# A Fourier mixing layer with a low-rank mixer: narrow products put side by side in four groups of partitions, and two small copies moved ahead of the weight loads

## The chip, the cores and the metric

The kernel runs on one core of one Trainium2 chip. The metric is device time in microseconds of one launch. The engines are named as the profile names them: PE is the matmul engine, with PEld for its loads of the stationary operand; DVE, ACT and POOL are the vector, scalar and general engines; SP issues DMAs. A matmul `out <- moving, stationary` of "98*128 98x425" contracts 98 partitions, has 128 stationary columns and 425 moving columns.

## The reference

For eight batches of 3136 positions by 256 channels:

```python
X = np.fft.fft(x, axis=1); X = np.fft.fft(X, axis=2); x = X.real     # (8, 3136, 256)
xt = x.transpose(0, 2, 1)
h = xt @ U @ V                          # over positions, rank 32
u = x + h.transpose(0, 2, 1)
out = u + np.maximum(u @ w_ch1, 0.0) @ w_ch2    # 256 -> 1024 -> 256
```

## The kernel before

**Transform.** The real part of the two-dimensional transform is written as cosine and sine sums. Per batch, DVE folds x over channels (`along_d`, L348) and over positions (`mirror`, L357; `half`, L361) into two tables `G` (`g`, one for each parity `par` of the output position). PE multiplies their columns with the position tables `tabs` (sine, typ 0) and `tabc` (cosine, typ 1) in `seq` (L423): one call for each parity, type and parity `pn` of the contracted position, each of four products of 425 moving columns: 393 output positions and 32 columns that carry the low-rank factor U. `halves` (L390) does a call with `pn` 0 from products of 229 columns and two DVE operations that make the rest of it by symmetry. ACT copies the `pn` 0 result to `ev`, and DVE adds and subtracts it to the `pn` 1 result, giving the arrays `A` (cosine) and `B` (sine) and the slice `tab` for the low rank. `even_ch`, `odd_ch` (L552, L561) transform over channels and make `S` and `T`; `across` (L569, L571) copies what is left over into `VA`. `lowrank` (L579) makes `TA`. PSUM tag `dft` with three buffers serves all of these.

**The channels that the folding leaves over.** Channel 0 folds with nothing and stands alone. For batches 0 and 1 it is column 256 of `G`, copied there by way of POOL (`alone`, L354), and its position transform is carried by four more products in each call of `seq` with typ 0 (L421), which add it as row 0 of `B`. With those, batch 1 can't use `halves` for typ 0. For the six batches from 2 on the channels are loaded apart by SP (`column_loads`) and transformed together in the *column pass* (`column_steps`): `fold_c` makes tables `GC`, `group` (L511) runs four times, for each `par` and `pn`, with four products of 6 stationary columns each, and `finish` makes `rows` and the low-rank part `tabc128`.

**Mixer.** The 25088 rows are taken in 49 chunks of 512. `front` (L612, L620) makes u; `first_product` (L632) and a ReLU on ACT (L634) make `h`; `second_product` (L648) and DVE (L654 to L657) make the output, which SP stores.

**Order.** Up to the end of chunk 0 everything is queued in the order in which it is written; after it a scheduler orders the instructions within engines, from a list `due` that spreads the steps of batch b+1's fold and transform over the chunks of batch b. In the setup, tables are made by ACT, POOL and DVE; `transform_u` (L274) already has 32-column products that write four groups of 32 partitions of one PSUM tile:

```python
nc.tensor.matmul(acc[g * R:(g + 1) * R, :], GU[:kp(i), typ, pn, i, :], ...)   # L274, g in range(4)
```

POOL's order around the moved copies is: four `mirror_even` copies (L309), `load_weights` (L55 gather of w, L195), `cosine_odd(4)` (L323), `alone(0, ...)` twice (L354), `load_v`, `g_zeros(0)`, batch 1's first load, `ta_rows`, `alone(1, ...)` twice, memsets, and later `channel_tables` (L807), which scales row 0 of `MC`.

Of the kernel before, what the change touches and what calls it, by code (L numbers as in the profile page):

```python
# [10 lines left out]
BF16 = mybir.dt.bfloat16  # L11
# [5 lines left out]
P = 128  # L17
# [10 lines left out]
def kernel(  # L28
# [153 lines left out]
    MSN = cpool.tile([P, 256], BF16, name="msn")  # L182
    MC = cpool.tile([P, 256], BF16, name="mc")
    ME = cpool.tile([P, P], BF16, name="me")
    MO = cpool.tile([P, P], BF16, name="mo")
    nc.vector.tensor_scalar(ncol[:], ncol[:], 1.0 / S, 0.0, op0=AL.mult, op1=AL.max)

    w1 = [gen.tile([P, H], FP32, name=f"w1{s}", tag=f"w1{s}", bufs=1) for s in range(2)]
# [210 lines left out]
    def seq(b, par, typ, pn, parts=(0, 1)):  # L399

        if b not in ST:
            d = ST[b] = {}
            d["A"] = wp.tile([P, HALF + 1], BF16, tag="A", name="A", bufs=1)
            d["B"] = wp.tile([P, HALF + 1], BF16, tag="B", name="B", bufs=1)
            d["S"] = wp.tile([P, HALF + 1], BF16, tag="S", name="S", bufs=2)
            d["T"] = wp.tile([P, HALF + 1], BF16, tag="T", name="T", bufs=2)
        d = ST[b]
        g = G[b % 2][par]
        if pn == 0 and (b >= B0 or (b == 1 and typ == 1)):
            halves(d, g, par, typ)  # L410
            return
        if 0 in parts:
            d[par, pn] = psum.tile([P, QW], FP32, tag="dft", name="pt", bufs=3)
        pt = d[par, pn]
        if typ == 1:
            mm = [(1, 128, i) for i in ktiles(pn)]
        else:
            mm = [(0, 0, i) for i in ktiles(pn)]
            if b < B0:
                mm += [(1, 256, i) for i in ktiles(1 - pn)]  # L420
        for n, (t, col, i) in enumerate(mm):  # L421
            if n // (NI // 2) in parts:
                nc.tensor.matmul(pt[:], g[:kp(i), i, col:col + P], tabs[t][:kp(i), i, par, :],  # L423
                                 start=(n == 0), stop=(n == len(mm) - 1))
        if 1 not in parts:
            return
        if pn == 0:
            ev = d["ev"] = wp.tile([P, QW], FP32, tag="ev", name="ev", bufs=2)
            nc.scalar.copy(ev[:], pt[:])
            return  # L430
        ev = d["ev"]
        nc.vector.tensor_tensor(TAB[:, (2 * typ + par) * R:(2 * typ + par + 1) * R],  # L432
                                pt[:, NQ:QW], ev[:, NQ:QW], op=AL.add)
        dst = d["A"] if typ == 1 else d["B"]
        if par == 0:
            up, c0 = dst[:, HALF // 2::-2], 0
        else:
            up, c0 = dst[:, HALF // 2 - 1:0:-2], 1
        dn = dst[:, HALF // 2 + 2 - par:HALF + 1 - par:2]
        nc.vector.tensor_tensor(up, pt[:, c0:NQ], ev[:, c0:NQ], op=AL.add)  # L440
        if typ == 1:
            nc.vector.tensor_tensor(dn, ev[:, 1:NQ], pt[:, 1:NQ], op=AL.subtract)
        else:
            nc.vector.tensor_tensor(dn, pt[:, 1:NQ], ev[:, 1:NQ], op=AL.subtract)
# [3 lines left out]
    NB = B - B0  # L448
    cf = cpool.tile([KP, 2, NI, NB], FP32, name="cf")
    cr = cpool.tile([KP, 2, NI, NB], FP32, name="cr")  # L450
    GC = [cpool.tile([KP, NI, NB], BF16, name=f"gc{par}", tag=f"gc{par}") for par in range(2)]
    rows = cpool.tile([NB, S], BF16, name="rows")
    tabc128 = cpool.tile([P, (NB + 3) * R], BF16, name="tabc128")
    flip = cpool.tile([P, 2, P], BF16, name="flip")
    unit = cpool.tile([P, NB], FP32, name="unit")

    def column_zeros():
        nc.gpsimd.memset(cf[:], 0.0)
        nc.gpsimd.memset(cr[:], 0.0)

    def column_flips():
        nc.vector.tensor_copy(flip[:], fl[:])
# [2 lines left out]
    def column_loads():  # L465

        for t, dst, n in ((0, cf, NI - 1), (1, cr, 0)):
# [7 lines left out]
            for b in range(NB):  # L475
                for a in range(2):
# [5 lines left out]
                                        [[8 * D, PQ], [D, NI]])))  # L482
                    yield load

    def column_steps():
        ec = cpool.tile([KP, 2, NI, NB], BF16, name="ec")
        tc_ = cpool.tile([NB, 2, R], FP32, name="tc")

        def fold_c():
# [9 lines left out]
                                 start=False, stop=(a == 1))  # L499
            nc.scalar.copy(ec[:], pc[:])  # L500
            for par in range(2):
                nc.vector.tensor_tensor(GC[par][:], ec[:, 0], ec[:, 1],
                                        op=AL.add if par == 0 else AL.subtract)
        yield fold_c
        ev = {}

        def group(par, pn):
            pt = psum.tile([NB, QW], FP32, tag="dft", name="ptc", bufs=3)
            ks = ktiles(pn)
            for n, i in enumerate(ks):  # L510
                nc.tensor.matmul(pt[:], GC[par][:kp(i), i, :], tabs[1][:kp(i), i, par, :],  # L511
                                 start=(n == 0), stop=(n == len(ks) - 1))
            if pn == 0:
                ev[par] = wp.tile([P, QW], FP32, tag="ev", name="evc", bufs=2)
                nc.scalar.copy(ev[par][:NB], pt[:])
                return
            e = ev[par][:NB]
            up = rows[:, HALF // 2 - par:(0 if par else None):-2]
            dn = rows[:, HALF // 2 + 2 - par:HALF + 1 - par:2]
            nc.vector.tensor_tensor(up, pt[:, par:NQ], e[:, par:NQ], op=AL.add)  # L520
            nc.vector.tensor_tensor(dn, e[:, 1:NQ], pt[:, 1:NQ], op=AL.subtract)
            nc.vector.tensor_tensor(tc_[:, par, :], pt[:, NQ:QW], e[:, NQ:QW], op=AL.add)
        for par in range(2):
            for pn in range(2):
                yield lambda par=par, pn=pn: group(par, pn)

        def finish():
            nc.scalar.copy(rows[:, HALF + 1:S], rows[:, HALF - 1:0:-1])
            nc.vector.tensor_tensor(tc_[:, 0], tc_[:, 0], tc_[:, 1], op=AL.add)
            for b in range(NB):  # L530
                nc.vector.tensor_single_scalar(tabc128[:NB, b * R:(b + 1) * R], tc_[:, 0],
                                               unit[:NB, b:b + 1], op=AL.mult)
        yield finish

    def chan(b, ch, h):
# [20 lines left out]
    def odd_ch(b, ch):  # L556
        d = ST[b]
        lo = ch * 392 + (1 if ch else 0)
        hi = (ch + 1) * 392 + 1
        pt = psum.tile([P, NQ], FP32, tag="dft", name="pst", bufs=3)  # L560
        nc.tensor.matmul(pt[:, :hi - lo], MO[:], d["B"][:, lo:hi], start=True, stop=True)  # L561
        for k, op in (("S", AL.add), ("T", AL.subtract)):
            nc.vector.tensor_tensor(d[k][:, lo:hi], d["e"][:, :hi - lo], pt[:, :hi - lo], op=op)  # L563

    def across(b, to, src, ch):

        lo = ch * 392 + (1 if ch else 0)
        hi = (ch + 1) * 392 + 1
        nc.scalar.copy(VA[b % 2][to, lo:hi], src[:, lo:hi])  # L569
        lo, hi = max(lo, 1), min(hi, HALF)  # L570
        nc.scalar.copy(VA[b % 2][to, S - hi + 1:S - lo + 1], src[:, hi - 1:lo - 1:-1])  # L571

    def lowrank(b):
        d = ST[b]
        pt = psum.tile([P, 256], FP32, tag="dft", name="ptt", bufs=3)
        n = 0
        for typ in range(2):
            for par in range(2):
                nc.tensor.matmul(pt[:], TAB[:, (2 * typ + par) * R:(2 * typ + par) * R + P],  # L579
                                 MDT[typ][:],  # L580
                                 start=(n == 0), stop=(n == 3 and b < B0))
                n += 1
        if b >= B0:
            nc.tensor.matmul(pt[:], tabc128[:, (b - B0) * R:(b - B0) * R + P], ones[:], start=False, stop=True)
            nc.sync.dma_start(out=VA[b % 2][R:R + 1, :], in_=rows[b - B0:b - B0 + 1, :])
        nc.scalar.copy(TA[b % 2][:R, :], pt[:R])

# [79 lines left out]
    def transform(b):  # L667

        for par, typ in ([(0, 0), (1, 0), (0, 1), (1, 1)] if b == 0 else
                         [(0, 1), (0, 0), (1, 1), (1, 0)]):  # L670
            for pn in range(2):
                yield lambda par=par, typ=typ, pn=pn: seq(b, par, typ, pn)
        if b == 0:
            for ch in range(4):
                for h in range(2):
                    yield lambda ch=ch, h=h: chan(b, ch, h)
            return
        for ch in range(4):
            yield lambda ch=ch: (even_ch(b, ch), across(b, slice(2 * R, P), ST[b]["A"][2 * R:], ch))
            yield lambda ch=ch: (odd_ch(b, ch),  # L680
                                 b < B0 and across(b, slice(R, R + 1), ST[b]["B"][0:1], ch))
        yield lambda: lowrank(b)

    CK = {}
# [26 lines left out]
            mirror_even(0, 3)  # L711
    cosine_low(1)
    mirror_even(0, 1)
    load_weights()
    cosine_odd(4)
    halve(0)
    for part in range(2):
        along_d(0, xr, EOR_, part)
# [32 lines left out]
        load_f(1, a)  # L751
        load_0(1, a, nc.sync)

    alone(0, xr, EOR_)
    alone(0, xf, EOF_)
    load_v()
    g_zeros(0)

# [4 lines left out]
    mirror(0, slice(128, 258), AL.add)  # L763
    load_second(0)
    ta_rows(0)
    alone(1, xr, EOR_)
    alone(1, xf, EOF_)
    uc[0]()
    busy(3)
    uc[1]()  # L770
# [29 lines left out]
    ta_rows(1)  # L800
    nc.gpsimd.memset(ones[:], 1.0)
    column_zeros()
    nc.gpsimd.memset(tabc128[:].bitcast(I32), 0)

    def channel_tables():

        nc.gpsimd.tensor_single_scalar(MC[0:1], MC[0:1], 0.5, op=AL.mult)  # L807
        nc.gpsimd.tensor_copy(ME[:], MC[:, :P])
        nc.gpsimd.memset(ME[QD:, 0:1], 0.0)
        nc.gpsimd.tensor_copy(MO[:], MSN[:, :P])  # L810
        nc.gpsimd.memset(MO[0:1], 0.0)

    early = ((0, 0), (0, 1), (1, 0))
    for par, pn in early:
# [21 lines left out]
    for step in steps[4:6]:  # L836
        step()

    due = {0: steps[6:7], 1: steps[7:8], 2: [lambda: last_row(0), column_flips]}

    def spread(steps, lo, hi):

# [59 lines left out]
```

## Time and profile before

| | |
|---|---|
| runs | 463.79 us median of 3 (462.05 to 465.17) |
| the profiled execution | 463.73 us; span 462.0 us |
| PE | 444.9 us busy, 2988 matmuls |
| DVE, ACT, POOL | 353.1, 299.8, 69.7 us busy |
| mean granted clock of PE | 0.996 |

The span runs from the first to the last instruction; the time of the execution is 1.7 us longer. Starts are in microseconds from the span's start. Matmuls overlap, so the step from one to the next is shorter than the duration of one. The setup lasts to about 38 us, when chunk 0's `front` comes.

### The profile page before, as it was taken

Reading aid. Unit: us, or ns where it says so; the run is one execution under the profiler, and the core shown is the slowest. Engines: PE = TensorE matmul, PEld = TensorE weight load, DVE = VectorE, ACT = ScalarE, POOL = GpSimd, SP = SyncE. Lnnn points to the kernel's source line nnn. Section 1 sums busy time; section 2 is a strip of 40 time slices with the busy share of each in tenths; the row PEclk is TensorE's granted clock in tenths of the full one; section 3 lists DMA queues with packets and bytes.
Section 4 is the critical chain, followed back from the end, with each engine's and each line's share of the span. In section 5 each row is a group of like instructions: output and inputs, shape, how many; then the busy total and the mean of one; then the engine's idle time right before and its main releaser. Section 6 shows DMA issues by size and latency. Waiting matters only on the chain.

```text
span 462.0 us, 8048 instructions
## 1 busy us (share of the span) xinstructions
PE 444.9 (96%) x2988; PEld 290.7 (63%) x2988; DVE 353.1 (76%) x811; ACT 299.8 (65%) x570; POOL 69.7 (15%) x112
## 2 busy tenths in 40 slices
PE   3889999899999999999999999999999999999996
PEld 2544656565666666666666666666666666666665
DVE  8887998886898779977898769977898666433433
ACT  7866537965876568655866577655865586656552
POOL 5992621020022001120022002100000000000000
PEclk9989999999999999999999999999999999999999
DMA  7994898994276824973377736683235323333343
GB/s 217 233 238 111 172 219 200 132 206 96 69 193 197 213 70 132 208 217 92 115 209 201 148 81 161 193 218 111 70 91 115 91 71 115 91 116 92 114 116 113
DMA packets 102955, 67.51 MB, mean 146 GB/s; under 512 B 73526, under 2 KB 99328, under 8 KB 99776
## 3 DMA queue, kind: packets, MB, share of 16 engines
q1 hardware_dynamic: 97906, 41.26, 38.3%
q0 software_dynamic: 4992, 25.74, 19.4%
q8 instruction: 23, 0.38, 0.3%
q14 instruction: 16, 0.13, 0.1%
q10 hardware_dynamic: 18, 0.00, 0.0%
HBM read 29.33 MB, written 25.69 MB: 119 GB/s over the span
## 4 chain that ended last, share of the span: by engine, by line
PE 87%; DVE 5%; POOL 2%; ACT 2%; issue 2%; DVEq 0%; POOLq 0%
PE p L648 35%; PE p L632 34%; PE pt L423 7%; PE ph L612 4%; PE pth L390 2%; DVE eor L348 1%; PE pst L561 1%; DVE eof L348 1%; PE pst L552 1%; DVE u L620 1%; PE ptt L579 1%; PE ptc L511 1%; DVE eos L357 1%; POOL xf L55 1%; ACT tabs L218 0%
## 5 line engine op out<-in xcount | busy, mean ns | idle before, releaser
L634 ACT ACTIVATE h<-p 128x512 bf16<-128x512 f32 x392 | 223.4, 597 | 130.3 <-PE p L632 128.4
L632 PE MATMUL p<-u,w 128*128 128x512 bf16 x784 | 218.8, 379 | 1.0 <-DVE u L620 0.8
L648 PE MATMUL p<-w,h 128*128 128x256 bf16 x1568 | 203.4, 273 | 0.0
L648 PEld LDWEIGHTS <-h 128*128 128x128 bf16 x1568 | 152.9, 98 | 59.9 <-issue 0.5
L632 PEld LDWEIGHTS <-w 128*128 128x128 bf16 x784 | 76.0, 98 | 52.4 <-issue 3.6
L654 DVE TENSOR_TENSOR o<-p,ut 128x4 f32<-128x4 f32 (+1 forms) x100 | 16.3, 163 | 58.8 <-PE p L648 56.3
L55 POOL DMA_INDIRECT xf<-in_x_dram,xidx x16 | 20.9, 1304 | 190.3 <-DVE eof L348 187.1
L657 DVE TENSOR_TENSOR o<-p,ut 128x254 f32<-128x254 f32 (+1 forms) x100 | 40.7, 407 | 0.0
L656 DVE TENSOR_TENSOR o<-p,ut 128x254 f32<-128x254 f32 (+1 forms) x100 | 40.7, 407 | 0.0
L348 DVE TENSOR_TENSOR eor<-xr 99x1024 bf16<-99x1024 f32 x32 | 39.1, 1230 | 0.0
L348 DVE TENSOR_TENSOR eof<-xf 99x1024 bf16<-99x1024 f32 x32 | 38.5, 1217 | 0.0
L620 DVE TENSOR_TENSOR u<-ph,S 128x512 bf16<-128x512 f32 (+15 forms) x64 | 35.1, 557 | 0.0
L620 DVE TENSOR_TENSOR u<-ph,T 128x512 bf16<-128x512 f32 (+15 forms) x64 | 35.0, 557 | 0.0
L423 PEld LDWEIGHTS <-g 98*128 98x128 bf16 (+1 forms) x184 | 18.3, 100 | 19.7 <-issue 2.3
L612 PE MATMUL ph<-va,ta 128*128 128x512 bf16 (+18 forms) x128 | 29.6, 329 | 0.6 <-ACT evd L554 0.6
L563 DVE TENSOR_TENSOR S<-evd,pst 128x392 bf16<-128x392 f32 (+1 forms) x28 | 15.8, 563 | 9.7 <-PE pst L561 7.8
L357 DVE TENSOR_TENSOR eos<-eof,eor 99x1024 bf16<-99x1024 bf16 (+2 forms) x33 | 21.9, 676 | 1.6 <-POOL eof L354 1.5
L423 PE MATMUL pt<-tabc,g 98*128 98x425 bf16 x104 | 22.2, 343 | 0.1
L423 PE MATMUL pt<-tabs,g 98*128 98x425 bf16 x80 | 19.1, 370 | 1.5 <-DVE g L361 1.5
L361 DVE TENSOR_TENSOR g<-eos 99x2048 bf16<-99x2048 bf16 (+3 forms) x20 | 19.8, 1008 | 0.2
L432 DVE TENSOR_TENSOR tab<-pt,ev 128x32 bf16<-128x32 f32 x32 | 6.1, 191 | 17.7 <-PE pt L423 16.7
L563 DVE TENSOR_TENSOR T<-evd,pst 128x392 bf16<-128x392 f32 (+1 forms) x28 | 15.7, 560 | 0.0
(157 smaller groups left out, 332.3 us busy)
## 6 DMA issues: line engine op xcount, KB each, us to landing
out_dram<-o SPq DMA_DIRECT2D x48, 512.0 KB
xr<-in_x_dram POOLq DMA_DIRECT2D x14, 784.0 KB, 6.3
xr<-in_x_dram SPq DMA_DIRECT2D x2, 784.0 KB
ut<-u SPq DMA_TRANSPOSE x49
w<-in_moe_w_ch_dram SPq DMA_DIRECT2D x1, 512.0 KB
w<-in_moe_w_ch_dram POOLq DMA_DIRECT2D x1, 512.0 KB, 5.7
out_dram<-o SPq DMA_DIRECT2D x4, 128.0 KB
va<-in_moe_V_dram POOLq DMA_DIRECT2D x2, 196.0 KB, 5.3
```

The lines of the kernel that those rows point to most:

```text
L55: nc.gpsimd.indirect_dma_start(out_, None, bass.AP(t.tensor, t.offset, [[w, rows], [1, w]]), bass.IndirectOffsetOnAxis(idx, 0), element_of ...
L348: pin(nc.vector.tensor_tensor(dst[:, a, :, part * P:(part + 1) * P].rearrange("p i (k t) -> p i k t", k=2), lo, hi, op=AL.subtract if part ...
L357: pin(nc.vector.tensor_tensor(EOS[:, a, :, cols], EOF_[:, a, :, cols], EOR_[:, a, ::-1][:, :, cols], op=op))
L423: nc.tensor.matmul(pt[:], g[:kp(i), i, col:col + P], tabs[t][:kp(i), i, par, :], start=(n == 0), stop=(n == len(mm) - 1))
L563: nc.vector.tensor_tensor(d[k][:, lo:hi], d["e"][:, :hi - lo], pt[:, :hi - lo], op=op)
L612: nc.tensor.matmul(ph[:, col:col + hi - lo], TA[b % 2][:, s * P:(s + 1) * P], VA[b % 2][:, lo:hi], start=True, stop=True)
L620: nc.vector.tensor_tensor(u[:, s, col:col + hi - lo], ph[:, col:col + hi - lo], src, op=AL.add)
L632: nc.tensor.matmul(p1[:], W1[:, s, j * P:(j + 1) * P], k["u"][:, s, :], start=(s == 0), stop=(s == 1))
L634: LAST[0] = nc.scalar.activation(k["h"][:, j, :], p1[:], AF.Relu)
L648: nc.tensor.matmul(p2[:, t % w, :], h[:, j, rs], W2[:, j, :], start=(j == 0), stop=(j == JT - 1))
L656: nc.vector.tensor_tensor(o[:, ts, 1:P], p2[:, :w, 1:P], ut[:, ts, 1:P], op=AL.add)
L657: nc.vector.tensor_tensor(o[:, ts, P + 1:D], p2[:, :w, P + 1:D], ut[:, tT, P - 1:0:-1], op=AL.add)
```

## The change

A new generator `narrow` runs the sixteen products of a narrow transform as one step: four groups (`pn`, `par`) write partitions 32g to 32g+31 of one PSUM tile in turn, with 32 stationary columns each. ACT copies the two `pn` 0 groups in one instruction, and DVE then makes the sums for both parities from slices of partitions.

- The column pass uses `narrow` in place of four `group` steps. `GC` becomes flat and gets 32 zero columns behind it, so that each product can take 32.
- Batch 1's single channel leaves `seq`: there, only batch 0 still has the extra products, and `halves` serves typ 0 of batch 1 too. `first_channel`, placed between batch 1's `seq` steps and its channel steps, transforms it with `narrow` from columns 256 to 287 of `G`, straight into row 32 of `VA[1]`; two ACT copies mirror it, and the copies of row 0 of `B` in `across` go. Its low-rank part goes to the table `low` (`tabc128` with one block more), and `lowrank` has one more product for batch 1.
- `MO` goes; `odd_ch` uses `MSN[:, :P]`, since row 0 of `B` is now zero.
- In the setup `alone(0, ...)` and `cosine_odd(4)` come ahead of `load_weights`, and `alone(1, ...)` comes where `alone(0, ...)` was.
- `column_flips` moves from `due` slot 2 to slot 44.

```diff
-        if pn == 0 and (b >= B0 or (b == 1 and typ == 1)):
+        if pn == 0 and b > 0:
             halves(d, g, par, typ)
...
-            if b < B0:
+            if b == 0:
                 mm += [(1, 256, i) for i in ktiles(1 - pn)]
...
-    GC = [cpool.tile([KP, NI, NB], BF16, name=f"gc{par}", tag=f"gc{par}") for par in range(2)]
+    GC = [cpool.tile([KP, NI * NB + R], BF16, name=f"gc{par}", tag=f"gc{par}") for par in range(2)]
...
+    def narrow(nb, stationary, dst, tc_):
+        t = {}
+        def products():
+            pt = t["pt"] = psum.tile([P, QW], FP32, tag="dft", name="ptc", bufs=3)
+            for n in range(NI // 2):
+                for g in range(4):
+                    pn, par = divmod(g, 2)
+                    i = ktiles(pn)[n]
+                    nc.tensor.matmul(pt[g * R:(g + 1) * R], stationary(par, i),
+                                     tabs[1][:kp(i), i, par, :],
+                                     start=(n == 0), stop=(n == NI // 2 - 1))
+            t["ev"] = wp.tile([P, QW], FP32, tag="ev", name="evc", bufs=2)
+            nc.scalar.copy(t["ev"][2 * R:], t["pt"][:2 * R])
+        yield products
+        def sums(par):
+            e, o = (t[k][(2 + par) * R:(2 + par) * R + nb] for k in ("ev", "pt"))
...
+            nc.vector.tensor_tensor(up, o[:, par:NQ], e[:, par:NQ], op=AL.add)
+            nc.vector.tensor_tensor(dn, e[:, 1:NQ], o[:, 1:NQ], op=AL.subtract)
+            nc.vector.tensor_tensor(tc_[:, par], o[:, NQ:QW], e[:, NQ:QW], op=AL.add)
+            if par:
+                nc.vector.tensor_tensor(tc_[:, 0], tc_[:, 0], tc_[:, 1], op=AL.add)
+        for par in range(2):
+            yield lambda par=par: sums(par)
...
+        yield from narrow(NB, lambda par, i: GC[par][:kp(i), i * NB:i * NB + R], rows, tc_)
...
+    def first_channel():
+        tc_ = cpool.tile([1, 2, R], FP32, name="tc1")
+        dst = VA[1][R:R + 1]
+        yield from narrow(1, lambda par, i: G[1][par][:kp(i), i, 256:256 + R], dst, tc_)
+        def finish():
+            mid = (HALF + S) // 2
+            for lo, hi in ((HALF + 1, mid), (mid, S)):
+                nc.scalar.copy(dst[:, lo:hi], dst[:, S - lo:S - hi:-1])
+            nc.vector.tensor_copy(low[:1, :R], tc_[:, 0])
+        yield finish
...
-        nc.tensor.matmul(pt[:, :hi - lo], MO[:], d["B"][:, lo:hi], start=True, stop=True)
+        nc.tensor.matmul(pt[:, :hi - lo], MSN[:, :P], d["B"][:, lo:hi], start=True, stop=True)
...
+        if b > 0:
+            nc.tensor.matmul(pt[:], low[:, (b - 1) * R:(b - 1) * R + P], ones[:], start=False,
+                             stop=True)
...
+        if b == 1:
+            yield from first_channel()
...
             yield lambda ch=ch: (odd_ch(b, ch),
-                                 b < B0 and across(b, slice(R, R + 1), ST[b]["B"][0:1], ch))
...
+    alone(0, xr, EOR_)
+    alone(0, xf, EOF_)
+    cosine_odd(4)
     load_weights()
-    cosine_odd(4)
...
-    alone(0, xr, EOR_)
-    alone(0, xf, EOF_)
+    alone(1, xr, EOR_)
+    alone(1, xf, EOF_)
     load_v()
...
-    due = {0: steps[6:7], 1: steps[7:8], 2: [lambda: last_row(0), column_flips]}
+    due = {0: steps[6:7], 1: steps[7:8], 2: [lambda: last_row(0)], 44: [column_flips]}
```

More of the change, by code (lines that the diff above doesn't have):

```diff
@@ L184 @@
     ME = cpool.tile([P, P], BF16, name="me")
-    MO = cpool.tile([P, P], BF16, name="mo")
     nc.vector.tensor_scalar(ncol[:], ncol[:], 1.0 / S, 0.0, op0=AL.mult, op1=AL.max)
@@ L450 @@
     cr = cpool.tile([KP, 2, NI, NB], FP32, name="cr")
-    GC = [cpool.tile([KP, NI, NB], BF16, name=f"gc{par}", tag=f"gc{par}") for par in range(2)]
+    GC = [cpool.tile([KP, NI * NB + R], BF16, name=f"gc{par}", tag=f"gc{par}") for par in range(2)]
     rows = cpool.tile([NB, S], BF16, name="rows")
-    tabc128 = cpool.tile([P, (NB + 3) * R], BF16, name="tabc128")
+    low = cpool.tile([P, (NB + 4) * R], BF16, name="low")
     flip = cpool.tile([P, 2, P], BF16, name="flip")
@@ L459, in column_zeros @@
         nc.gpsimd.memset(cr[:], 0.0)
+        for par in range(2):
+            nc.gpsimd.memset(GC[par][:, NI * NB:], 0.0)
     def column_flips():
@@ L483, in column_loads @@
                     yield load
+    def narrow(nb, stationary, dst, tc_):
[14 more added lines that the diff above has]
+            e, o = (t[k][(2 + par) * R:(2 + par) * R + nb] for k in ("ev", "pt"))
+            up = dst[:, HALF // 2 - par:(0 if par else None):-2]
+            dn = dst[:, HALF // 2 + 2 - par:HALF + 1 - par:2]
+            nc.vector.tensor_tensor(up, o[:, par:NQ], e[:, par:NQ], op=AL.add)
[3 more added lines that the diff above has]
+                nc.vector.tensor_tensor(tc_[:, 0], tc_[:, 0], tc_[:, 1], op=AL.add)
+        for par in range(2):
+            yield lambda par=par: sums(par)
     def column_steps():
@@ L501, in fold_c @@
             for par in range(2):
-                nc.vector.tensor_tensor(GC[par][:], ec[:, 0], ec[:, 1],
+                nc.vector.tensor_tensor(GC[par][:, :NI * NB].rearrange("p (i b) -> p i b", b=NB), ec[:, 0], ec[:, 1],
                                         op=AL.add if par == 0 else AL.subtract)
         yield fold_c
[L505 to L522, printed above, removed]
@@ L523, in column_steps @@
-        for par in range(2):
-            for pn in range(2):
-                yield lambda par=par, pn=pn: group(par, pn)
+        yield from narrow(NB, lambda par, i: GC[par][:kp(i), i * NB:i * NB + R], rows, tc_)
         def finish():
             nc.scalar.copy(rows[:, HALF + 1:S], rows[:, HALF - 1:0:-1])
-            nc.vector.tensor_tensor(tc_[:, 0], tc_[:, 0], tc_[:, 1], op=AL.add)
             for b in range(NB):
-                nc.vector.tensor_single_scalar(tabc128[:NB, b * R:(b + 1) * R], tc_[:, 0],
+                nc.vector.tensor_single_scalar(low[:NB, (b + 1) * R:(b + 2) * R], tc_[:, 0],
@@ L560, in odd_ch, with across @@
         pt = psum.tile([P, NQ], FP32, tag="dft", name="pst", bufs=3)
-        nc.tensor.matmul(pt[:, :hi - lo], MO[:], d["B"][:, lo:hi], start=True, stop=True)
+        nc.tensor.matmul(pt[:, :hi - lo], MSN[:, :P], d["B"][:, lo:hi], start=True, stop=True)
         for k, op in (("S", AL.add), ("T", AL.subtract)):
             nc.vector.tensor_tensor(d[k][:, lo:hi], d["e"][:, :hi - lo], pt[:, :hi - lo], op=op)
-    def across(b, to, src, ch):
+    def across(b, ch):
+        to, src = VA[b % 2][2 * R:], ST[b]["A"][2 * R:]
         lo = ch * 392 + (1 if ch else 0)
         hi = (ch + 1) * 392 + 1
-        nc.scalar.copy(VA[b % 2][to, lo:hi], src[:, lo:hi])
+        nc.scalar.copy(to[:, lo:hi], src[:, lo:hi])
         lo, hi = max(lo, 1), min(hi, HALF)
-        nc.scalar.copy(VA[b % 2][to, S - hi + 1:S - lo + 1], src[:, hi - 1:lo - 1:-1])
+        nc.scalar.copy(to[:, S - hi + 1:S - lo + 1], src[:, hi - 1:lo - 1:-1])
     def lowrank(b):
@@ L580, in lowrank @@
                                  MDT[typ][:],
-                                 start=(n == 0), stop=(n == 3 and b < B0))
+                                 start=(n == 0), stop=(n == 3 and b == 0))
                 n += 1
+        if b > 0:
+            nc.tensor.matmul(pt[:], low[:, (b - 1) * R:(b - 1) * R + P], ones[:], start=False,
+                             stop=True)
         if b >= B0:
-            nc.tensor.matmul(pt[:], tabc128[:, (b - B0) * R:(b - B0) * R + P], ones[:], start=False, stop=True)
             nc.sync.dma_start(out=VA[b % 2][R:R + 1, :], in_=rows[b - B0:b - B0 + 1, :])
@@ L678, in transform @@
         for ch in range(4):
-            yield lambda ch=ch: (even_ch(b, ch), across(b, slice(2 * R, P), ST[b]["A"][2 * R:], ch))
-            yield lambda ch=ch: (odd_ch(b, ch),
-                                 b < B0 and across(b, slice(R, R + 1), ST[b]["B"][0:1], ch))
+            yield lambda ch=ch: (even_ch(b, ch), across(b, ch))
+            yield lambda ch=ch: odd_ch(b, ch)
         yield lambda: lowrank(b)
@@ L765 @@
     ta_rows(0)
-    alone(1, xr, EOR_)
-    alone(1, xf, EOF_)
     uc[0]()
@@ L802 @@
     column_zeros()
-    nc.gpsimd.memset(tabc128[:].bitcast(I32), 0)
+    nc.gpsimd.memset(low[:].bitcast(I32), 0)
     def channel_tables():
@@ L809, in channel_tables @@
         nc.gpsimd.memset(ME[QD:, 0:1], 0.0)
-        nc.gpsimd.tensor_copy(MO[:], MSN[:, :P])
-        nc.gpsimd.memset(MO[0:1], 0.0)
     early = ((0, 0), (0, 1), (1, 0))
```

## The prediction

> **What bounds the kernel now.** I read the page's totals first, then the busy time by stretches of 15 us, then the chain that ended last, then the timelines of single engines around the places where the change sits.
>
> ```profile
> PE 444.9 (96%) x2988; PEld 290.7 (63%) x2988; DVE 353.1 (76%) x811; ACT 299.8 (65%) x570; POOL 69.7 (15%) x112
> ```
>
> The matmul engine is busy for 96% of the span, so in most stages time goes only with PE work. By stretches (columns: stretch and its length, then busy us of PE, PEld, DVE, ACT, POOL; granted clock, DMA share, GB/s):
>
> ```profile
> 60.00:75.00 15.00, 14.31 (x88) 8.45 (x89) 14.86 (x30) 5.87 (x12) 2.19 (x4) 1.00 0.93 204
> 75.00:90.00 15.00, 13.21 (x88) 8.46 (x87) 11.18 (x27) 14.65 (x31) 1.08 (x2) 1.00 0.87 143
> 90.00:105.00 15.00, 14.96 (x108) 10.09 (x106) 12.56 (x26) 9.75 (x21) 3.37 (x4) 1.00 0.98 216
> 105.00:120.00 15.00, 15.00 (x94) 8.03 (x91) 10.90 (x37) 8.02 (x15) 0.00 (x0) 1.00 0.37 88
> ```
>
> Batch 1's transform lies in 60 to 90 us, where PE stands for 0.69 + 1.79 us in all, first beside a full DVE, then beside a full ACT. The column pass lies in 105 to 120 us under a full PE. From 90 us on PE hardly pauses: what is saved there is saved at the end. Before 45 us it is otherwise. Timelines of POOL, DVE and PE (start, length, what; in brackets the idle time before it and who ended it), and PE's granted clock (third number):
>
> ```profile
> 17.07 1.27 POOL L55 DMA_INDIRECT w<-in_moe_w_ch_dram,pint  x1 [0.16 <-issue]
> 18.35 0.62 POOL L195 DMA_DIRECT2D w<-in_moe_w_ch_dram  x1
> 18.94 0.89 POOL L323 COPY tabc<-tabs 99x784 bf16<-99x784 bf16 x1
> 19.73 0.26 POOL L354 CAST eor<-xr 99x8 bf16<-99x8 f32 x1
> 19.86 0.26 POOL L354 CAST eof<-xf 99x8 bf16<-99x8 f32 x1
> ...
> 20.15 0.70 DVE L357 TENSOR_TENSOR eos<-eof,eor 99x1040 bf16<-99x1040 bf16 x1 [1.23 <-POOL eof L354]
> ...
> 24.83 4.02 PE L423 MATMUL pt<-tabs,g 98*128 98x425 bf16 x12 [1.47 <-DVE g L361]
> 28.68 2.33 PE L423 MATMUL pt<-tabc,g 98*128 98x425 bf16 x12
> ...
> 25.00:28.90 3.90, 3.90 (x14) 0.56 0.90 240
> ```
>
> DVE idles 1.23 us for two small POOL copies (`alone`, L354) that stand behind the weight loads; this delays `g`, so PE gets its first transform products 1.47 us late, and then runs the first twelve at half clock: twelve take as long as 4.02 us where the next twelve take 2.33.
>
> **The change part by part.** Prices of PE work come from the chain (start, length, what), where a length is the step to the next instruction:
>
> ```profile
> 116.34 0.82 PE ptc L511 x4
> 117.16 0.54 PE p L632 x2
> ...
> 118.57 0.43 PE p L632 x2
> 119.00 0.72 PE pt L423 x4
> ...
> 121.91 0.40 PE pth L390 x4
> ```
>
> Four full-width products cost 0.72, four short ones (`halves`) 0.40. Four of the column pass's 6-wide ones cost 0.82, and the two L632 behind them 0.54 where two cost 0.43 elsewhere: 0.10 on the way in and 0.11 on the way out, 0.93 a group. Products in four groups side by side exist already, at L274:
>
> ```profile
> 20.99 0.85 PE L274 MATMUL pu<-tabc,gu 98*32 98x393 bf16 x16 [0.32 <-ACT tabc L311]
> 21.78 0.67 PE L732 MATMUL idle<-tabs 98*128 98x393 bf16 x3
> ```
>
> Sixteen of 393 columns take 0.79 to the next plain product, way out included. For 425 columns 0.79 x 425/393 = 0.85, with the way in 0.95 a burst.
>
> *Column pass.* Four groups of 0.93 = 3.72 become one burst of 0.95: 2.77 saved, under a PE that never stops. ACT loses one `evc` copy (0.50), DVE does the same sums in the same sizes.
>
> *Batch 1's single channel.* The 16 products that carried it (L421) go, and eight more full-width ones become eight short ones: 24 x 0.18 = 4.32 less, 2 x 0.40 = 0.80 more, a burst 0.95 more, and one more product in `lowrank` 0.11 more (four cost 0.44 there): 2.46 saved on PE. ACT: the eight copies of row `B` (L569, L571; eight at 0.42 apart = 3.4) go, two half-row copies come (0.8 each, from L528's 1.50 for a whole row), `evc` (0.50) comes, two `ev` shrink from 0.52 to 0.35: about 1.6 less in the stretch where ACT was full. DVE: two more pairs of `halves` sums (0.35 and 0.40, with the wait between them 0.9 a pair) and the narrow sums (four at 0.48 apart, two of 0.11, two of 0.18): 4.2 more, in a stretch (60 to 105 us) where DVE was idle for 6.4 of 45.
>
> Whether PE keeps the 2.46 I settled by walking the built program's queues with these durations from 61.8 us on (old times). PE meets no wait until 75.3; the `ptc` burst gets its buffer when DVE has read `ph` (74.5, burst at 74.6). ACT's copies of `A` then run from 71.8 to 75.6 and `evc` ends at 76.1; DVE comes to the narrow sums at 78.1, ends them at 80.3. PE waits 0.3 for `evd` (77.6), 0.85 for the output sums L654 that DVE now reaches later (83.0), 0.4 for them again (92.5), and small ones; in all about 2.4, against 2.52 before in the same 45 us. So stalls change places and the 2.46 stay. Bounds: no stall left, 5.0; all new DVE work exposed, 2.46 - 4.2 = -1.7.
>
> *Single channels of batch 0 ahead of the weights.* POOL can do the two copies at 16.95 to 17.4, then L323, the weights (gather from 18.3), then batch 0's second pair of copies, V, the zeros of `g` (done by 22.6 instead of 22.1). DVE goes on at 18.94 instead of 20.15, so `g` comes at 22.9 to 24.2; the second pair, moved up as well, takes away the 0.25 that DVE waited for it at 25.6. PE is free at 23.2 and starts at 23.6. I take it that with a gap of 0.4 instead of 1.47 the clock stays whole. Then 32 products end at 29.4; buffers freed by DVE and ACT, and ACT's `weights(1)` (2.06), spread the last 16 to 32.6; DVE ends `A` at 34.0, not 36.9. What ends last now is POOL's scaling of `mc` (L807, 33.7 before), which stays put but for two small memsets (0.1 each, less the 0.1 of overlap) ahead of it: its product L579 goes from 36.18 to about 33.95. Gain 2.2. With the half clock still there 1.2 is left; if x lands too late for POOL at 17, nothing. Loads moved back: weights by 1.3, V by 0.6, batch 1's x by 0.7. Weights land at about 24 (4.4 after their gather) and are cast at 28.6, V is read at 36, x at 42; a cover that failed would cost those figures.
>
> [...]
>
> *Small things.* `column_flips` (0.45 on DVE) moves from 43.1 to behind an `eos` at 47: DVE is full on both sides, nothing. `MO` goes (0.55 of idle POOL). No DMA is added; SP's queue swaps one `rows` copy with one output store.
>
> Sum: 2.2 + 2.46 + 2.77 = 7.4 off the profiled execution's 463.73 (span 462.0 and 1.7 around it), which is the runs' median of 463.79 within their spread: **456.3 us**.
>
> [...] Loads of 32 columns take 95 ns and of 128 columns 98, but fifteen of them lay within 0.45 us at L274. Were they one behind the other, a burst would take 16 x 0.095 = 1.5 and the time would be 457.6.
>
> **The rivals.**
> *DVE becomes the bound of batch 1.* For it: DVE at 14.86 of 15 in 60 to 75 us, and 4.2 us more work. Against: the 6.4 us idle behind it. All exposed: 2.2 - 1.7 + 2.77 = 3.3 saved, 460.5.
> *The groups don't run side by side.* [...] Against: L274 does exactly this, with the same moving table.
> *The setup gains nothing*, the rest does: 458.5. For it: arrival of x is not shown, only that DVE read it unhindered at 15.3 and 20.8.
> *Slower: ACT's queue blocks PE.* ACT has eight `A` copies (3.4) queued ahead of `evc`; behind `evc` stand `h` and `evd`; DVE stands at the narrow sums and cannot free `ptc`. The walk gives 2.0 us of slack (76.1 against 78.1). If `A` comes later than that, PE, with three `dft` buffers, stops at each of the next three (`pst`). A stop of 1.5 as at 24.83 brings 3.4 us of half clock: 1.5 + 1.7 = 3.2, three times 9.6: 465.9. Against: 1.15 was the longest stop there and kept the clock.
>
> **How the numbers follow.** The forecast with its own spread (454 to 458.8, the setup's three values within it) 0.72; DVE bound 0.16; not side by side 0.04; ACT's queue 0.08. About 1% (4.6 us) is what a measurement of this kernel can tell from no change: the first is faster, the next two within 1%, the last slower. The range goes from 453.6 (2.2 + 5.0 + 2.8 saved, rounded) to 461.2, past both cases in the middle.
>
> **What would show it.** Right: DVE's wait for `eof` L354 gone, L423 starting near 23.6 at clock 1.00, L579 near 34; each `ptc` burst 0.85 to 0.95 long; PE idle in 58 to 103 us still 2 to 3 us; PE's busy total down by some 5. Wrong: the half clock still there, PE waits of over 1.2 us for ACT or DVE in batch 1, a burst of 1.5 or more, or a DVE without idle time until 100 us.

## The result, and the profile after

| | before | after |
|---|---|---|
| median of 8 runs | 463.77 us (462.05 to 465.17) | 459.17 us (457.91 to 462.07) |
| profiled execution, span | 463.73, 462.0 us | 458.82, 457.0 us |
| mean granted clock there | 0.996 | 1.000 |

The ratio is 0.9914, with a 95% interval from 0.9884 to 0.9943: faster by 4.6 us in the medians and by 4.9 in the profiled executions, where 7.4 was forecast. The lines that answer to those shown of the kernel before, first the totals:

```profile
PE 436.8 (96%) x2937; PEld 288.9 (63%) x2989; DVE 356.8 (78%) x823; ACT 296.3 (65%) x564; POOL 66.7 (15%) x112
```

PE has 8.1 us less busy time, 1.7 of it the half clock that this execution doesn't have, and some of it records that are missing (2937 matmuls against 2989 weight loads). By stretches of 15 us (busy of PE, PEld, DVE, ACT, POOL; clock, DMA share, GB/s):

```profile
60.00:75.00 15.00, 14.68 (x113) 9.82 (x115) 14.89 (x35) 9.59 (x21) 1.57 (x2) 1.00 0.81 172
75.00:90.00 15.00, 14.14 (x88) 8.42 (x88) 14.88 (x33) 10.96 (x22) 1.96 (x3) 1.00 0.86 140
90.00:105.00 15.00, 13.51 (x101) 8.29 (x101) 12.62 (x31) 7.93 (x17) 1.78 (x4) 1.00 1.00 224
105.00:120.00 15.00, 14.89 (x106) 9.99 (x105) 13.58 (x44) 11.55 (x22) 0.00 (x0) 1.00 0.31 96
```

DVE is now full from 60 to 90 us, and yet PE stands for 0.32 + 0.86 there, less than before. Between 90 and 105 PE stands for 1.5 us where it hardly stood. Then the setup, in the timelines of POOL, DVE and PE (start, length, what; in brackets the idle time and who ended it), with the granted clock in the same stretch as before:

```profile
16.86 0.67 POOL L353 CAST eor<-xr 99x8 bf16<-99x8 f32 x1
17.45 0.42 POOL L353 CAST eof<-xf 99x8 bf16<-99x8 f32 x1
17.78 1.86 POOL L322 COPY tabc<-tabs 99x784 bf16<-99x784 bf16 x1
19.80 1.28 POOL L55 DMA_INDIRECT w<-in_moe_w_ch_dram,pint  x1 [0.16 <-issue]
...
23.72 1.00 POOL L164 MEMSET g<- 99x504 int32 x2
...
19.05 1.15 DVE L356 TENSOR_TENSOR eos<-eof,eor 99x1040 bf16<-99x1040 bf16 x1
...
24.30 1.29 DVE L360 TENSOR_TENSOR g<-eos 99x1024 bf16<-99x1024 bf16 x2 [1.01 <-POOL g L164]
...
25.04 2.34 PE L422 MATMUL pt<-tabs,g 98*128 98x425 bf16 x12 [1.38 <-DVE g L360]
...
35.31 0.38 PE L601 MATMUL ptt<-mc,tab 128*128 128x256 bf16 x2 [0.41 <-POOL mc L832]
...
25.00:28.90 3.90, 3.86 (x22) 2.10 (x23) 3.83 (x7) 2.16 (x3) 3.39 (x8) 1.00 1.03 229
```

DVE no longer waits for `eof`, as forecast, but the wait is not gone: it stands 4 us later, at `g`, for the zeros that POOL writes there. PE starts no earlier (25.04 against 24.83), but at whole clock. Last, the two bursts and what lies around the second, with the copy `cb` on ACT:

```profile
73.75 0.91 PE L496 MATMUL ptc<-tabc,g 98*32 98x425 bf16 x16
...
101.96 0.27 ACT L523 CAST cb<-cr 99x96 bf16<-99x96 f32 x1 [0.91 <-DMA cr<-in_x_dram]
...
102.28 0.23 PE L528 MATMUL pc<-cb,flip 99*99 99x48 bf16 x2 [0.86 <-ACT cb L523]
...
104.11 0.91 PE L496 MATMUL ptc<-tabc,gc 98*32 98x425 bf16 x16
104.95 0.61 PE L656 MATMUL p<-u,w 128*128 128x512 bf16 x2
```

In the kernel before, PE did not wait there:

```profile
104.30 0.23 PE L498 MATMUL pc<-cb,flip 99*99 99x48 bf16 x2
```

A burst takes 0.84 to the next product, in the forecast 0.85. Four marks on PE tell where the 4.9 us came from: the product of `mc` (L579, now L601), the wait for chunk 3's `u` near 59 us, the first `pth` of batch 2, and the short `ph` (128x97) behind the column pass.

| start, us | `mc` product | `u` | first `pth` | `ph` 128x97 |
|---|---|---|---|---|
| before | 36.18 | 60.32 | 104.69 | 120.87 |
| after | 35.31 | 59.33 | 102.46 | 115.95 |
| before, with fillers (below) | 34.87 | 59.02 | 103.38 | 119.56 |
| best version (below) | 34.87 | 59.03 | 101.18 | 114.67 |

Between the first two rows the kernel gained: setup 1.0, batch 1 1.2, column pass 2.7. Forecast: 2.2, 2.46 and 2.77.

### The profile page after: what moved, and what is told of

The parts are those of the page before. It is cut to its first block, busy times and chain, and to the rows that moved or that the text cites. A ratio compares the mean times of both kernels' runs of the same rounds, so it can differ in the third digit from the quotient of the medians.

```text
span 457.0 us, 8003 instructions
## 1 busy us (share of the span) xinstructions
PE 436.8 (96%) x2937; PEld 288.9 (63%) x2989; DVE 356.8 (78%) x823; ACT 296.3 (65%) x564; POOL 66.7 (15%) x112
## 4 chain that ended last, share of the span: by engine, by line
PE 77%; DVE 9%; POOL 5%; issue 4%; SPq 1%; ACT 1%; DMA 1%; DVEq 0%; POOLq 0%; ACTq 0%
PE p L672 33%; PE p L656 30%; PE ph L636 4%; PE pt L422 4%; PE pth L389 2%; DVE eor L347 1%; DVE eof L347 1%; DVE u L644 1%; SPq L480 1%; PE pst L573 1%; DMA cr<-in_x_dram 1%; POOL xf L55 1%; PE pst L582 1%; PE ptt L601 1%; DVE A L441 1%
## 5 line engine op out<-in xcount | busy, mean ns | idle before, releaser
L656 PE MATMUL p<-u,w 128*128 128x512 bf16 x735 | 208.5, 379 | 2.2 <-DVE u L644 1.0
L55 POOL DMA_INDIRECT xf<-in_x_dram,xidx x16 | 19.5, 1216 | 185.3 <-DVE eof L347 172.7
L636 PE MATMUL ph<-va,ta 128*128 128x512 bf16 (+13 forms) x125 | 29.2, 328 | 0.2
L422 PEld LDWEIGHTS <-g 98*128 98x128 bf16 (+1 forms) x160 | 15.5, 97 | 16.3 <-DVE g L360 1.5
L422 PE MATMUL pt<-tabc,g 98*128 98x425 bf16 x88 | 18.7, 343 | 0.1
L422 PE MATMUL pt<-tabs,g 98*128 98x425 bf16 x72 | 15.6, 344 | 1.4 <-DVE g L360 1.4
```

The source lines that it names most:

```text
L55: nc.gpsimd.indirect_dma_start(out_, None, bass.AP(t.tensor, t.offset, [[w, rows], [1, w]]), bass.IndirectOffsetOnAxis(idx, 0), element_of ...
L636: nc.tensor.matmul(ph[:, col:col + hi - lo], TA[b % 2][:, s * P:(s + 1) * P], VA[b % 2][:, lo:hi], start=True, stop=True)
L656: nc.tensor.matmul(p1[:], W1[:, s, j * P:(j + 1) * P], k["u"][:, s, :], start=(s == 0), stop=(s == 1))
```

## The experiments

**First set: the parts by themselves.** The setup undone:

```diff
-    alone(0, xr, EOR_); alone(0, xf, EOF_); cosine_odd(4); load_weights()
+    load_weights(); cosine_odd(4)
...
-    alone(1, xr, EOR_); alone(1, xf, EOF_); load_v()
+    alone(0, xr, EOR_); alone(0, xf, EOF_); load_v()
...
+    alone(1, xr, EOR_); alone(1, xf, EOF_)     # behind ta_rows(0)
```

> The changed kernel with the three edits of the setup undone: the small copies of batch 0 (`alone`) again behind the weight loads and `cosine_odd(4)`, the second pair behind the loads of batch 1. Theory A (the wait only moved from the copies to the zeros of `g`, and what is left is POOL's scaling of `mc` coming earlier): the setup is worth the 1.0 us by which the chunk's `u` came earlier at 59 us in the trace, so 459.2 + 1.0 = 460.2; `g` again near 24.1, the product of `mc` again near 36.2. Theory B (the setup gave its 2.2 us as forecast, and the other parts fell short): 461.4. Theory C (the moved copies give nothing at all, what the trace shows is chance): 459.2.

Measured: 460.29 us (457.28 to 464.54; 459.76 without the longest run, whose clock was 0.989), ratio to before 0.990 [0.986, 0.994]. That is near theory A's 460.2 with all runs and between theories A and C without the longest; six runs spread too widely to choose. Most of the spread goes with the clock: the run at 1.000 had 457.28, those at 0.996 459.67 and 459.76, that at 0.993 462.47; one at 0.991 had 460.83, out of this order.

Column pass alone (setup and batch 1's channel taken back as well, by the lines of the diff above):

> The kernel before with only the column pass as narrow products in four groups of partitions; setup and batch 1's single channel as before. Theory A: the column pass is worth what the marks of the two traces say, 2.7 us: 463.8 - 2.7 = 461.1, PE's `ptc` products in one burst of about 0.85 and 0.95 with the ways in and out. Batch 1's channel is then the difference to the run with the setup undone, 460.2 against 461.1, so 0.9 to 1.2. Theory B (the column pass gave less, and batch 1's channel its full 2.46): 462.5 or more, since 4.9 - 1.0 - 2.46 = 1.4 would be left for it.

Measured: 460.25 us, ratio 0.9915 [0.9881, 0.9948], the same as with the setup undone, and again in steps of the clock: 459.35 and 459.40 at 1.000, about 461.1 at 0.996. Against the 462.1 to 462.6 of the kernel before at 1.000 that is 2.7 to 3.2: theory A for the column pass. In its profile the way from the first `pth` to the short `ph` is 13.49 (105.09 to 118.58) where it was 16.18: 2.69 by the column pass alone. The price of batch 1's channel can't be read from medians that depend on how many runs the half clock caught. At equal clock the two kernels of this set differ by 2.1 at 1.000 (457.28, a single run, against 459.35 and 459.40) and by 1.4 at 0.996.

The zeros of `g` early:

```diff
     nc.gpsimd.memset(pint[0:1], P)
+    g_zeros(0)
...
     load_v()
-    g_zeros(0)
```

> The changed kernel with the zeros of `g` (two memsets, 1.0 us on POOL) moved up into POOL's idle time from 7.8 to 11.8 us. Theory A (what kept PE waiting at 25.04 is these zeros, 1.01 us on DVE): DVE's wait for POOL's `g` is gone, `g` comes right after `eos` at 23.3 to 24.6, PE starts near 23.9, everything POOL issues behind `load_v` comes 1.0 earlier, the product of `mc` at about 34.3, and the time falls by 1.0 to 458.2. With a gap of under 0.5 us ahead of the first products the clock is whole in each run (before and after, with gaps of 1.4 to 1.5, some runs show a mean clock of 1.000 and some of 0.993 to 0.996, and the latter are longer), so the spread of the runs shrinks too. Theory B (the start is not what decides, but `cosine` of `mc` and POOL's scaling, or the loads of batch 1's x): PE starts earlier and waits later, 459.2. Theory C (the reduced clock is a matter of chance and not of the gap): clocks below 1.000 show up in some of these runs as well.

Measured: 459.03 us (457.23 to 459.96), five of six clocks at 0.996. The wait for POOL's zeros was gone and PE waited no more for `mc`, but PE started at 24.94, not at 23.9. Theory A failed on that; the time is near theory B's 459.2, though PE didn't start early, as that theory had it. PE stood for 2.02 ahead of its start, so whether a gap under 0.5 keeps the clock was not tested here. The timeline of DVE in that run:

```profile
8.15 0.75 DVE L211 TENSOR_SCALAR phe<-krow,ncol 99x394 f32<-99x394 f32 x1
8.94 0.64 DVE L213 TENSOR_SCALAR phe<-phe 99x394 int32<-99x394 int32 x1
...
17.46 1.34 DVE L357 TENSOR_TENSOR eos<-eof,eor 99x1024 bf16<-99x1024 bf16 x1
...
24.19 1.29 DVE L361 TENSOR_TENSOR g<-eos 99x1024 bf16<-99x1024 bf16 x2
```

DVE stands for 0.45 in all from 7 us to `g` (1.37 in the changed kernel); it is the chain that sets the start. Beside the moved zeros its two `phe` operations took 0.75 and 0.64, where the same two take 0.41 and 0.37 in the changed kernel, and beside L323, which POOL began at 17.42, `eos` took 1.34, not 0.88. Here DVE paid for what POOL did early.

Groups in turn:

```diff
-            for n in range(NI // 2):
-                for g in range(4):
+            for g in range(4):
+                for n in range(NI // 2):
```

> The changed kernel with the sixteen products of each narrow burst in another order: one group of partitions after the other (four products each) in place of the four groups in turn. Same products, same results. Theory A (products of neighbouring groups run beside one another, those of one group don't): a burst takes 16 x 0.18 = 2.9 where it took 0.84, so 2.0 more, twice, the one in batch 1 partly under a full DVE: 461 to 463.3. Theory B (the saving is from the smaller partition count alone and not from their running side by side): no change, 459.2.

Measured: 459.37 us, ratio to before 0.9904 [0.9874, 0.9934], and both bursts nearly as short as they were (0.87 to the next product); the second one on PE:

```profile
102.62 0.94 PE L496 MATMUL ptc<-tabc,gc 98*32 98x425 bf16 x16
103.49 0.60 PE L656 MATMUL p<-u,w 128*128 128x512 bf16 x2
```

Theory A's number failed, theory B's came; which of the two mechanisms it is was settled in the third set.

**Second set: the clock.** Twelve filler products behind the setup's last ones, in both kernels:

```diff
     uc[2]()
+    busy(12)
```

> The kernel before with twelve filler products (2.0 us at whole clock, results not used) behind the last products of the setup and ahead of the transform of batch 0, where PE stands idle for 1.4 to 2.9 us. So far the runs of one kernel differ by their mean clock: the thirteen of before lie at 462.1 to 462.6 (clock 1.000), 463.7 to 464.3 (0.996) and 465.2 to 465.7 (0.993), and the profiled ones show one or two stretches of 3.4 us at half clock right behind this pause. Theory A (the pause brings the half clock, and which run gets it hangs on when the clock first rose): with the pause filled, all runs have a clock of 0.999 or more and lie at 462 to 462.8, the median 1.4 below 463.7. Theory B (the half clock falls by chance whatever PE does there): clocks of 0.993 to 0.996 in more than half of the runs, median 463.7.

Measured: 462.45 us (462.42 to 463.63) in twelve runs, all at 0.998 to 1.000. None had the half clock, which ten of the thirteen runs of before in the first set had. Theory A for the clock. The ratio to before, 0.9982 [0.9962, 1.0001], doesn't exclude no change, since many runs of before have the whole clock too: it is the spread that shrank.

> The changed kernel with the same twelve filler products in the same place. Theory A: all clocks 0.999 or more, times 457.9 to 458.9, median 458.4 (the four undisturbed runs of the changed kernel had 457.9, 458.6, 458.7, 458.8), so the change is worth 3.8 at whole clock, against 462.2 of the kernel before with fillers, and not the 4.9 that the two profiled executions showed, of which 1.7 was the half clock of the one before. Theory B (chance): median 459.2, clocks as before. A filler that ends after `g` has come would cost up to 0.6 at the start, which the later wait for `mc` takes back.

Measured: 458.64 us in seven runs, ratio to before 0.9888 [0.9857, 0.9919]; six lie at 457.87 to 459.03 with clocks of 0.998 to 1.000. The seventh (464.49) is the profiled one, and its half clock lies elsewhere (0.61 granted from 105 to 110 us), behind this:

```profile
103.90 1.46 PE L656 MATMUL p<-u,w 128*128 128x512 bf16 x3 [4.44 <-DVE u L644]
```

PE stood for 4.44 us for a `u` that DVE made late, since DVE itself stood 5.24 ahead of the output sums that read the transposed `ut`. The profile names no releaser for that; an earlier `ut` of this run took 10.3 us from its issue at 76.68 to its landing among the column loads, so a late transpose is likely, but this wasn't tried. Theory A holds for the pause it was about. Between 462.45 and the six, the change is worth some 4 us at whole clock.

**Third set: the new wait, and the groups.** Column loads five slots earlier:

```diff
-        due.setdefault(8 + 5 * n // 4, []).append(step)
+        due.setdefault(3 + 5 * n // 4, []).append(step)
```

> The changed kernel with the 28 loads of the column pass five slots (about 5 us) earlier in the queue. Theory A (PE's new wait of 0.86 and 0.17 us ahead of the products of `pc` is ACT's copy `cb`, which waits for the last of these loads): the wait is gone, 1.0 us less, 458.2. Theory B (the load only ends where the DMA engines, 0.8 to 1.0 busy, let it, or the stop comes back at the next buffer): 459.2.

Measured: 458.99 us (457.28 to 468.67; 458.62 without the longest, whose clock was 0.982), ratio 0.9886 [0.985, 0.9923]: between the two theories. In its profile PE's wait at L528 for `cb` is gone, but another one stands a little ahead of it:

```profile
102.95 1.18 PE L656 MATMUL p<-u,w 128*128 128x512 bf16 x4 [0.70 <-DVE u L644]
```

From the `u` mark to the first `pth` this profile has 43.18 us, as the changed kernel (43.13): nothing gained. With the clock out of the way, below, the earlier loads do show.

Thirteen products in one group:

```diff
-            for n in range(NI // 2):
-                for g in range(4):
-                    pn, par = divmod(g, 2)
-                    i = ktiles(pn)[n]
+            for g, count in ((0, 13), (1, 1), (2, 1), (3, 1)):
+                pn, par = divmod(g, 2)
+                for n in range(count):
+                    i = ktiles(pn)[n % 4]
```

> The changed kernel with thirteen of the sixteen products of each narrow burst put into the first group of partitions and one into each other group: the same number and size of products, but the sums of the single channels are not the reference's. Theory A (the groups work beside one another, even where four products of one group are issued in a row, as the run with the groups in turn showed): thirteen in one group take 13 x 0.18 = 2.3, a burst 2.4 to 2.6 where it took 0.85 to 0.95. Theory B (a product of 32 columns is in itself four times as fast as one of 128, wherever it lies): the burst stays at 0.85 to 0.95.

Measured (one run, 462.74 us at a clock of 0.993), in the timeline of PE:

```profile
106.43 2.53 PE L496 MATMUL ptc<-tabc,gc 98*32 98x425 bf16 x16
108.89 0.60 PE L656 MATMUL p<-u,w 128*128 128x512 bf16 x2
```

2.46 to the next product: theory A. A product of 32 columns is no faster than a wide one in its own group (2.46 / 13 = 0.19, against 0.18); different groups overlap, and with the groups in turn (0.87) they did so even with four products of one group ahead of the next group's in the queue.

**Fourth set: the setup at whole clock, and a version that is faster.** The fillers with the setup undone:

> The changed kernel with the setup as it was before and the twelve filler products: column pass and batch 1's channel alone, at whole clock. With fillers the kernel before has 462.45, the changed one about 458.5 in its undisturbed runs. Theory A (the move of the copies costs rather than gains: with fillers PE starts at 25.2 to 25.5 in both, and then the product of `mc` comes at 34.87 without a wait in the kernel before, and at 35.36 behind POOL's scaling in the changed one): 458.0, the product of `mc` near 34.9. Theory B (the moved copies gain 1.0 once the clock is taken out): 459.5.

Measured: 458.04 us (457.52 to 459.20), the product of `mc` at 34.94: theory A. With the setup's move the same kernel had it at 35.36 and some 458.5. The medians differ by about 0.5, within the spread of the runs, and the two marks by 0.42. But the profile of the groups in turn, with the same moved setup at whole clock, has the product of `mc` at 34.73, so that the move costs a little is not shown. That it gains 1.0 (theory B) is excluded: that would be 459.5. Then zeros and loads early, with nine fillers:

> The changed kernel with the zeros of `g` in POOL's idle time, the column loads five slots earlier, and nine filler products (1.5 us; twelve ended up to 0.5 behind `g`). Theory A (three separate small losses: the half clock, POOL's scaling of `mc` late behind the zeros, the copy `cb` late behind the loads): no wait of PE for `mc`, the product near 34.5, and 457.0, 1.5 below the changed kernel with fillers. Theory B (what is gained before 60 us is lost at the later waits for `u` and `o`, which hang on DVE): 458.4.

> The same as the run before this one, but with the setup's order of the kernel before, in which the zeros of `g` end ahead of DVE's need anyway. Theory A (with the zeros out of the way the moved copies are worth about what DVE waits for them, 0.25 to 0.5 in the profile with the setup undone): 457.4. Theory B (they were worth the forecast 1.2 to 2.2): 458.5 or more. Theory C (nothing): 457.0.

Measured: 457.37 us (ten of eleven runs at 457.21 to 457.91, one at 463.94 with a clock of 0.993) and 457.24 us (457.14 to 457.62 in six runs; ratio to before 0.9878 [0.9853, 0.9903]). Theory A of the first and theory C of the second: once PE is kept busy and the loads come in time, the move of the copies, with the zeros moved too, is worth nothing. Between 458.04 and 457.24 only the place of the loads and three fillers differ: the earlier loads are worth about 0.8 here. The second is the best version, 1.9 below the changed kernel in the medians and 1.4 below that of its four runs at whole clock (457.91 to 458.82). In its profile DVE waits for `eof` as it did in the kernel before:

```profile
20.14 0.70 DVE L356 TENSOR_TENSOR eos<-eof,eor 99x1040 bf16<-99x1040 bf16 x1 [1.20 <-POOL eof L353]
...
25.19 2.33 PE L422 MATMUL pt<-tabs,g 98*128 98x425 bf16 x12
...
34.87 0.38 PE L601 MATMUL ptt<-mc,tab 128*128 128x256 bf16 x2
...
101.00 0.23 PE L528 MATMUL pc<-cb,flip 99*99 99x48 bf16 x2
```

## Why the prediction was right, and where it was wrong

**Right: the direction, the range, and the two narrow transforms.** The cleanest comparison is that of the last two rows of the marks, where the setup is the same and the clock whole in both: batch 1 gains 103.38 - 101.18 = 2.20, the column pass (119.56 - 114.67) - 2.20 = 2.69. The terms were 2.46 and 2.77. The groups do run side by side (0.84 a burst), and a DVE that is full from 60 to 90 us does not bound PE. One of the walk's stops came as forecast, that for the output sums (0.78 at 82.19, forecast 0.85). The sign "a DVE without idle time until 100 us" was to speak against the forecast; it came, and PE stood no longer for it: the working by queues was right there and the sign was badly chosen. (DVE's new work in it adds up to 4.3, not 4.2, and the lower end of the range to 453.7; neither matters.)

**Mis-sized: batch 1's term, in the changed kernel as it is.** It got 1.2 of 2.46. The walk took stalls to change places at no cost, and it had the column loads landed. In the profile the products of `pc` waited 0.17 + 0.86 us for `cb`, and `cb` waited for `cr`, which these loads fill. The fold came one to two microseconds earlier, and the loads kept their slots; SP's queue was even done with them later, at 97.24 where it was 92.36.

How much is lost differs from one execution to the next. From the `u` mark to the first `pth` the kernel before takes 44.37, with fillers 44.36. The new batch 1 with the loads in their old place takes 44.00 (setup undone), 43.45 (the same with fillers), 43.19 (zeros early), 43.13 (the changed kernel) and 42.23 (groups in turn): a gain of 0.4 to 2.1. The 2.1 is the one profile of these in which ACT did not stand ahead of its copy of `cr`. With the loads five slots earlier both profiles with fillers have 2.2, the one without has 1.2, since PE stood for `u` instead. So the term of the forecast is there when the loads have landed; what makes them and `u` late in some executions stays open.

**Wrong: the setup's term, 2.2.** Three of its steps failed.

*"POOL can do the two copies at 16.95 to 17.4, then L323."* They were priced by rows (0.26 each, and 0.89 for L323) in which DVE stood idle, waiting for these very copies. Moved, they run beside a working DVE and took 0.67, 0.42 and 1.86, and the second `eos` took 1.15, not 0.70. The weights' gather came at 19.80 where the working had 18.3, the zeros of `g` ended at 24.7, not 22.6, and `g` waited 1.01 for them. So a wait of 1.23 was traded for a stretch of 0.45 and a wait of 1.01. L322 ran from 17.78 to 19.64, and until 18.94 DVE's `along_d` ran beside it; what of its 1.86 that accounts for was not shown.

In two other profiles with the moved setup, those of the groups in turn and of thirteen in one group, the stretch was milder: L322 took 1.30, the zeros ended at 23.74 and 23.87, and `g` did not wait for them. Even so PE started at 24.50 and 24.54, not at 23.6.

*"What ends last now is POOL's scaling of `mc` (L807, 33.7 before), which stays put ..."* It sits behind the same zeros and moved from 32.81 to 34.39. With the clock whole it is what PE waits for (0.41 at 35.31).

*"I take it that with a gap of 0.4 instead of 1.47 the clock stays whole."* The gap stayed (1.38), and the clock was whole by chance: four of the eight runs had it at 0.993 to 0.996. The 1.0 us of setup gain in the two profiled executions is a half clock of 1.7 that only the one of before had, less a loss of some 0.7. By the same `u` mark at whole clock the moved setup loses 0.4 between the two kernels with fillers and some 0.1 in the groups in turn (58.74 against 60.32 - 1.7). No run shows a gain from it of more than 0.2. That the pause brings the half clock was right: with fillers in it the kernel before had 0.998 to 1.000 in twelve runs.

## What to carry to other kernels

Before pricing a change at an idle gap of PE, find out whether the runs of the kernel differ by their mean clock; if they do, a few filler products in the gap make the runs comparable: those of the best version lie within 0.5 us, those of the kernel before in the same set within 3.3. One profile of each kernel is not enough either: with the same moved setup PE's first transform products came 0.6 us apart (24.50 to 25.08), and the same batch 1 took up to 1.8 us more or less. Price a copy that is moved on POOL by a row in which DVE is as busy as it will be at the new place (0.26 each beside an idle DVE here, 0.67 and 0.42 beside a busy one). When work on the critical engine shrinks, look for the loads that were placed to arrive just in time for the old pace.

## What the runs showed of the hardware

**The clock.** PE's first products of the launch take about twice as long as the later ones, with the granted clock shown as 1.00 there (5 to 16 us in both kernels). In the timelines of PE, a pair of `pf` products takes 1.06 (0.85 to the next) and then 0.59 (0.43 to the next). The step from one to the other comes at another moment in each execution (10.8 to 13.9 us in ten profiles); in the kernel before and in the changed one it lies here:

```profile
11.48 0.65 PE L248 MATMUL pf<-ur,nfl 99*99 99x256 f32 x2
```

```profile
13.19 0.70 PE L247 MATMUL pf<-ur,fl 99*99 99x256 f32 x2
```

With the later step, in the changed kernel, the last eight products of the setup began at 22.74, not 22.44, and PE stood for 1.38 ahead of `g`, not 1.47. In the kernel before the granted clock fell to 0.50 at about 25.25 and was 1.00 again at 28.65: a stretch of 3.40, and 13.65 us from the step near 11.6 to the fall. Pauses of 1.47 (before), 2.02 (zeros early) and 2.41 us (column pass alone) were followed by one stretch of about 3.4, of 1.73 (loads early), 2.17 (one group) and 2.87 (setup undone) by 6.8, as long as two; that of 1.38 in the changed kernel by none. The five other profiles have the fall about 13.6 behind the step too (the step worked out from the shortened pair, the fall from the granted clock in stretches of 2 us).

The length of the pause alone does not order these counts; its place does. In the three with one stretch PE's products began 0.1 to 0.6 ahead of the fall (24.83 against 25.25, 24.94 against 25.52, 25.22 against 25.32), in the three with two 0.1 to 0.7 behind it (25.08 against 24.86, 24.54 against 24.42, 25.32 against 24.59). A pause that reached past the fall went with a second stretch. That is a reading of six traces; no run moved the pause alone.

In time that is 0, 1.7 or 3.2 us: most runs of the kernel before have 462.1, 463.7 and 465.3 at mean clocks of 1.000, 0.996 and 0.993.

**The groups.** Sixteen products in four groups take 0.84 to 0.87 in either order of issue, thirteen in one group with three beside them 2.46.
